# A retention layer and a gated MLP on one core: four more state products as row tiles, k loaded as bf16, stores on a second queue, a new order

## The chip, the core and the metric

The kernel runs on one core of a Trainium2 chip. A core has five engines, each with its own instruction queue that is worked off in order: TensorE (PE: matmuls; its weight loads stand as PEld in the profile), VectorE (DVE), ScalarE (ACT), GpSimd (POOL) and SyncE (SP, which here only issues transfers). They wait for each other through semaphores. Matmuls write to PSUM, eight banks of 128 x 2 KB; the other data lie in SBUF. Transfers run on DMA engines; SP, ScalarE and GpSimd can issue them, and only GpSimd's queue can change the type on the way.

The metric is the device time in microseconds of one execution. The time before is 232.23 us, the median of three runs (232.0 to 232.47).

## What is computed

Two stages, cut to what matters:

```python
# q, k, v: [4 batches, 8 heads, 768 steps, 64]; gamma[h] = 1 - 2**(-5-h)
for t in range(768):
    state = gamma * state + outer(k[t], v[t])         # per batch and head, 64 x 64
    y[t] = (1 / sqrt(64)) * q[t] @ state
x = y as [3072 tokens, 512]
xn = x / sqrt(mean(x * x) + 1e-6) * rms_g
out = (silu(xn @ w_gate) * (xn @ w_val)) @ w_out      # 512 -> 1536 -> 512
```

The inputs and the output are float32 in memory.

## The kernel before

The 768 steps are cut into six chunks (c, 0 to 5) of 128; there are four batches (b, 0 to 3). For each chunk and batch: load q, k and v with decay factors put into them, transpose q and k, form the scores of the chunk (A, L405: 64 rows each, so two heads stand above each other in the array as row tiles), multiply them by a mask on VectorE (M, L427), and add the product of masked scores with v to the product of q with the state of all chunks before (Y, L442 and L446). The state is kept as float32 in `st_f` and as bf16 in `st_b`; K (L529) is k times v, U adds it, B copies it to bf16 on GpSimd. Then the norm: S (square sum, ScalarE, L459), R (the power -1/2, GpSimd, L469 and L471), N (VectorE, L483), and XE transposes the result into `xnT`.

When a chunk's four batches are there (512 tokens), the MLP runs over it: for each of 12 tiles of d_ff, g and v (L553, 4 matmuls of 512 columns each), s (silu on ScalarE, L563), h (the product on VectorE, L571); then for each batch d (12 matmuls, L578), o (copy from PSUM, L145) and st (the store, L591). The MLP of one chunk and the attention of the next are interleaved.

Nothing is scheduled by a compiler. A string ORDER lists some 870 steps; each engine does its own in the order in which they stand there. A step is `name.arguments/banks@engine`, so `A.2.2/7231` makes the scores of chunk 2, batches 2 and 3, in banks 7, 2, 3 and 1, and `st.0.0@S` stores from SP's queue. A step that writes a bank waits until the readers of what was there are done. Names that the change touches:

- Y, plain: 8 matmuls of 128x64 (L442) and 4 of 128x128 (L446), the state as a block diagonal. Where Z stands (L409 to L420; before, for chunk 4, batches 2 and 3 alone), the state product of two batches is made first, as 16 matmuls of 64x64 on row tiles (L418): even heads of both batches in one bank, odd heads in another. Y with a third argument then adds the rest to both banks (L437). S then takes two square sums of 256 columns for each batch (L456), R adds the halves, N writes two halves (L480).
- Lq, Lk, Lv: loads. From SP's queue they bring float32 into a ring (`qf`, `kf`, `vf`); from GpSimd's queue bf16. Ck copies k to bf16 (`kb`), Cq and V put the decay factors into q and v and make bf16 of them. V on ScalarE is 8 instructions (L358), on VectorE or GpSimd one (L360).
- tq, tk: transposes by transfer, from SP's queue.
- H: filler matmuls (L239), 512 columns each, of ones, whose result nobody reads.

Chunk 2's loads wait for the last piece of w_out (`("wo", 8)`); the weights come through GpSimd's queue as bf16, in five pieces each for w_gate and w_val.

Of the kernel before, what the change touches and what calls it, by code (L numbers as in the profile page):

```python
# [22 lines left out]
J.0.3/5 D.0.1@D wv.2.4 R.0.1 X.0.2/6 N.0.1 S.0.0 wg.2.4 A.0.3/41 R.0.0 X.0.1/0 XE.0.2@A wg.4.6 D.0.3@D M0.0.3
XE.0.1@A g.0.0.2.2.3/2 K.0.2.2/5 K.0.0.2/6 M1.0.3 U.0.2.2@A s.0.0.2.2.3 N.0.0 v.0.0.2.2.3/7 g.0.0.2.1.2/0
h.0.0.2.2.3 Y.0.3/5 Lq.1.0@P wv.4.6 X.0.0/3 U.0.0.2@A S.0.3 wg.6.9 Tk.1.1/4 v.0.0.2.1.2/2 XE.0.0@D s.0.0.2.1.2
h.0.0.2.1.2 g.0.0.2.0.1/6 R.0.3 wv.6.9 Ek.1.1@A v.0.3.4.0.3/3 v.0.2.3.0.3/4 N.0.3 g.0.3.4.0.3/0 Lk.1.2@P
s.0.0.2.0.1 X.0.3/6 v.0.0.2.0.1/5 XE.0.3@A Lk.1.0@P B.0.0 wg.9.12 s.0.3.4.0.3 Lq.1.1@P g.0.5.6.0.3/1
g.0.2.3.0.3/7 h.0.3.4.0.3 s.0.2.3.0.3 Lq.1.2@P h.0.2.3.0.3 g.0.4.5.0.3/0 wv.9.12 h.0.0.2.0.1 s.0.4.5.0.3
v.0.0.4.3.4/2 g.0.0.4.3.4/7 v.0.4.5.0.3/3 mc.1@P s.0.5.6.0.3 s.0.0.4.3.4 h.0.0.4.3.4 wo.0.4 v.0.5.6.0.3/4
h.0.5.6.0.3 D.1.1@P Lv.1.1@P h.0.4.5.0.3 Lv.1.0@P g.0.8.9.0.4/7 g.0.6.7.0.4/0 mc.0@D s.0.8.9.0.4 v.0.4.6.3.4/4  # L30
g.0.4.6.3.4/5 s.0.4.6.3.4 v.0.8.9.0.4/6 D.1.0@D D.1.2@P wo.4.8 s.0.6.7.0.4 Tk.1.2/2 Ek.1.2@D Tq.1.0/5
g.0.7.8.0.4/1 Eq.1.0@D h.0.8.9.0.4 v.0.6.7.0.4/7 h.0.4.6.3.4 wo.8.12 v.0.7.8.0.4/3 Lk.2.2@S s.0.7.8.0.4
h.0.6.7.0.4 g.0.11.12.0.4/5 s.0.11.12.0.4 Tk.1.0/7 h.0.7.8.0.4 Lk.2.0@S Tq.1.1/0 Lv.1.2@P Lq.1.3@P Tq.1.2/3
Eq.1.1@D B.0.1 Eq.1.2@D g.0.9.10.0.4/4 s.0.9.10.0.4 B.0.2 g.0.10.11.0.4/2 s.0.10.11.0.4 Ek.1.0@D A.1.0/3710
M1.1.1 A.1.2/46 v.0.10.11.0.4/2 v.0.11.12.0.4/0 M0.1.2 M0.1.1 v.0.9.10.0.4/5 M0.1.0 Lv.2.0@S d.0.0.0.4/1 M1.1.0
M1.1.2 h.0.9.10.0.4 Y.1.1/3 d.0.3.0.4/6 Lk.2.3@S h.0.11.12.0.4 Y.1.0/4 S.1.1 Lk.1.3@P R.1.1 h.0.10.11.0.4 S.1.0
N.1.1 d.0.1.0.4/0 R.1.0 d.0.2.0.4/5 N.1.0 X.1.1/3 d.0.2.4.8 d.0.0.4.8 Lv.1.3@P d.0.3.4.8 X.1.0/7 d.0.3.8.12
XE.1.0@A Y.1.2/2 Tq.1.3/7 d.0.0.8.12 S.1.2 d.0.1.4.8 Lq.2.0@S XE.1.1@D o.0.0@A Eq.1.3@D o.0.3@A R.1.2 N.1.2
Tk.1.3/1 d.0.2.8.12 X.1.2/3 Ek.1.3@A Ck.2.2@P D.1.3@D Lq.2.1@S A.1.3/17 XE.1.2@A M1.1.3 K.1.0/4 K.1.2.2/6
K.1.1/2 B.0.3 M0.1.3 Lq.2.2@S tk.2.2 Ck.2.0@A g.1.0.1.0.3/3 v.1.2.3.0.3/7 U.1.1@D Y.1.3/1 s.1.0.1.0.3  # L40
g.1.1.2.0.3/3 S.1.3 Lk.2.1@S g.1.3.4.0.3/2 o.0.2@A R.1.3 U.1.2.2@D d.0.1.8.12 Cq.2.1@P s.1.3.4.0.3 U.1.0@D
g.1.2.3.0.3/2 v.1.0.1.0.3/5 N.1.3 Lq.3.1@S s.1.1.2.0.3 X.1.3/3 h.1.0.1.0.3 tk.2.0 v.1.3.4.0.3/1 Lk.3.1@S tq.2.1
v.1.1.2.0.3/5 B.1.2 XE.1.3@D h.1.3.4.0.3 Ck.2.3@D s.1.2.3.0.3 h.1.2.3.0.3 h.1.1.2.0.3 g.1.9.10.0.4/4
v.1.9.10.0.4/6 tk.2.3 v.1.0.4.3.4/7 g.1.8.9.0.4/2 Cq.2.0@P Lq.2.3@S o.0.1@D s.1.9.10.0.4 V.2.0@D tq.2.0 Ck.2.1@D
g.1.0.4.3.4/0 B.1.0 v.1.8.9.0.4/5 h.1.9.10.0.4 Cq.2.2@P Lq.3.0@S s.1.0.4.3.4 g.1.11.12.0.4/1 tk.2.1 s.1.8.9.0.4
h.1.0.4.3.4 g.1.5.6.0.4/7 Lv.2.1@S B.1.1 h.1.8.9.0.4 v.1.5.6.0.4/0 s.1.5.6.0.4 g.1.4.5.0.4/4 Ck.3.1@A
g.1.10.11.0.4/5 Cq.3.1@D Lv.2.2@S v.1.11.12.0.4/7 Cq.2.3@P h.1.5.6.0.4 s.1.11.12.0.4 B.1.3 h.1.11.12.0.4
v.1.10.11.0.4/0 s.1.10.11.0.4 s.1.4.5.0.4 h.1.10.11.0.4 v.1.4.5.0.4/4 Cq.3.0@P h.1.4.5.0.4 g.1.7.8.0.4/5
Lk.3.0@S A.2.0/4726 tq.2.3 tq.2.2 M0.2.0 v.1.7.8.0.4/0 Lv.2.3@S tq.3.1 Lk.3.2@S M0.2.1 s.1.7.8.0.4 M1.2.1
g.1.6.7.0.4/1 h.1.7.8.0.4 M1.2.0 V.2.1@P v.1.6.7.0.4/5 Y.2.1/4 Ck.3.0@A s.1.6.7.0.4 S.2.1 K.2.1/0 tk.3.1 K.2.0/6  # L50
V.2.2@P h.1.6.7.0.4 A.2.2/7231 M0.2.3 d.1.1.0.10/5 Lk.3.3@S V.2.3@P M1.2.3 tq.3.0 M1.2.2 d.1.1.10.12 R.2.1
# [588 lines left out]
```

## Time and profile before

| | |
|---|---|
| median of three runs | 232.23 us |
| span of the profiled execution | 230.7 us |
| what lies around the span (median less span) | 1.5 us |
| TensorE busy | 223.7 us, 97% |
| VectorE, GpSimd, ScalarE busy | 128.7, 92.8, 87.8 us |
| bytes moved | 33.60 MB |
| q1 (transfers issued by SP): share of 16 engines | 51.0% |
| q0 (issued by GpSimd): share of 16 engines | 30.3% |

The profiled execution is one more execution; its own time is known by its span, from the first to the last instruction of the program, and the 1.5 us are taken as what lies around it.

How to read the profile: a row of a group has the line, the engine, the operation, what it writes and reads, the shapes and the number of instructions; then busy us in total and the mean ns of one; then the idle time of the engine ahead of them, and what ended it. The view of waits has who waited for whom: us in total, times, the longest. The chain of waits goes from the last instruction back to what released it, step by step; its rows here have start, length and what. In the timeline, a row has start, length, engine, line and operation; matmuls are pipelined, so the length of one holds a tail that overlaps the next, and the pitch is read from start to start.

### The profile page before, as it was taken

How to read it: one execution, taken by the hardware profiler on the slowest of the kernel's cores; microseconds unless marked ns; L12 is line 12 of the kernel's file. 1: busy time of each engine (PE TensorE's matmuls, PEld its weight loads, DVE VectorE, ACT ScalarE, POOL GpSimd, SP SyncE). 2: the span in 40 equal slices, each digit the busy share in tenths (PEclk: the TensorE clock that was granted, in tenths of full speed). 3: DMA queues.
4: the chain of work that ended last, by engine and by line, in shares of the span. 5: the costliest groups of instructions: out<-in, count | busy, mean ns of one | idle time of the engine just before them, and what ended most of it. 6: DMA issues, size and time to landing. Idle time of an engine off the chain costs nothing.

```text
span 230.7 us, 4733 instructions
## 1 busy us (share of the span) xinstructions
PE 223.7 (97%) x1822; PEld 119.3 (52%) x1849; DVE 128.7 (56%) x239; ACT 87.8 (38%) x197; POOL 92.8 (40%) x163
## 2 busy tenths in 40 slices
PE   8989999999999999999999999999999999999994
PEld 2567755556564554445544445544554444444552
DVE  5797296937574876476670648856664325432200
ACT  6776524216424450344420435661354124222021
POOL 8979999124866235424349401339040000000000
PEclk9999999999999999999999999999999999999999
DMA  7999999999978946999999989774216200001142
GB/s 132 158 175 122 187 174 192 201 185 239 180 164 186 203 104 172 245 162 248 231 141 263 216 194 227 155 117 99 65 23 190 108 0 0 0 12 38 45 180 93
DMA packets 105353, 33.60 MB, mean 146 GB/s; under 512 B 94450, under 2 KB 102386, under 8 KB 105331
## 3 DMA queue, kind: packets, MB, share of 16 engines
q1 hardware_dynamic: 81858, 25.70, 51.0%
q0 software_dynamic: 23472, 7.60, 30.3%
q8 instruction: 14, 0.23, 0.4%
q14 instruction: 9, 0.07, 0.1%
HBM read 28.31 MB, written 6.29 MB: 150 GB/s over the span
## 4 chain that ended last, share of the span: by engine, by line
PE 93%; DMA 3%; issue 1%; DVE 1%; ACT 0%; POOL 0%; DVEq 0%
PE v_ps L553 26%; PE g_ps L553 26%; PE o_ps L578 26%; DMA wg_b<-in_moe_w_gate_dram 3%; PE hot_ps L239 3%; PE a_ps L405 3%; PE y_ps L442 2%; PE y_ps L446 2%; PE o_ps L600 1%; PE kv_ps L529 1%; PE t_ps L368 1%; PE t_ps L373 1%; DVE am L427 1%; PE xt_ps L496 1%; PE g_row_ps L295 0%
## 5 line engine op out<-in xcount | busy, mean ns | idle before, releaser
L571 DVE TENSOR_TENSOR hT<-sg,v_ps 128x512 bf16<-128x512 bf16 (+2 forms) x76 | 48.0, 655 | 54.4 <-PE v_ps L553 39.8
L563 ACT ACTIVATE sg<-g_ps 128x512 bf16<-128x512 f32 (+2 forms) x76 | 42.4, 575 | 88.8 <-PE g_ps L553 79.1
L553 PE MATMUL g_ps<-xnT,wg_b 128*128 128x512 bf16 (+2 forms) x334 | 70.2, 343 | 0.8 <-DMA wg_b<-in_moe_w_gate_dram 0.4
L553 PE MATMUL v_ps<-xnT,wv_b 128*128 128x512 bf16 (+2 forms) x338 | 70.4, 344 | 0.5 <-issue 0.2
L578 PE MATMUL o_ps<-wo_b,hT 128*128 128x512 bf16 x265 | 62.3, 379 | 0.6 <-issue 0.2
L553 PEld LDWEIGHTS <-wg_b 128*128 128x128 bf16 x344 | 30.6, 98 | 30.3 <-DMA wg_b<-in_moe_w_gate_dram 0.8
L553 PEld LDWEIGHTS <-wv_b 128*128 128x128 bf16 x344 | 30.5, 98 | 29.1 <-DVE hT L571 0.2
L578 PEld LDWEIGHTS <-hT 128*128 128x128 bf16 x276 | 26.3, 98 | 29.7 <-DVE hT L571 0.2
L469 POOL TENSOR_SCALAR ms<-ssq 128x1 f32<-128x1 f32 x24 | 4.5, 189 | 48.8 <-ACT xsq L459 48.0
L427 DVE TENSOR_TENSOR am<-a_ps,causal 128x512 bf16<-128x512 f32 x32 | 20.2, 682 | 3.3 <-PE a_ps L405 3.2
L483 DVE SCALAR_TENSOR_TENSOR xn<-y_ps,rstd,g_bc 128x512 bf16<-128x512 f32 x22 | 16.4, 748 | 9.8 <-POOL rstd L471 8.0
L545 POOL CAST st_b<-st_f 64x256 bf16<-64x256 f32 x40 | 18.7, 467 | 6.7 <-DVE st_f L538 5.4
L459 ACT ACTIVATE xsq<-y_ps 128x512 f32<-128x512 f32 x22 | 13.1, 598 | 15.6 <-PE y_ps L446 14.2
L341 POOL TENSOR_TENSOR qb<-qf,ydec 128x512 bf16<-128x512 f32 x13 | 13.7, 1055 | 10.5 <-DMA qf<-in_q_dram 10.2
L145 ACT COPY o_sb<-o_ps 128x512 f32<-128x512 f32 (+1 forms) x15 | 8.4, 567 | 23.5 <-PE o_ps L578 23.1
L471 POOL TENSOR_TENSOR rstd<-ms,mhalf 128x1 f32<-128x1 f32 x24 | 13.2, 552 | 2.0
L145 DVE COPY o_sb<-o_ps 128x512 f32<-128x512 f32 (+2 forms) x11 | 6.7, 620 | 13.0 <-PE o_ps L578 7.3
L360 POOL TENSOR_TENSOR vp<-vf,vdec 128x512 bf16<-128x512 f32 x9 | 9.3, 1040 | 5.4 <-DMA vf<-in_v_dram 5.3
L427 DVE TENSOR_TENSOR am<-a_ps,mask 128x512 bf16<-128x512 f32 x16 | 9.9, 681 | 1.6 <-PE a_ps L405 1.4
L239 PE MATMUL hot_ps<-one 128*128 128x512 bf16 x23 | 8.4, 516 | 1.1 <-DVE one L152 1.1
L442 PEld LDWEIGHTS <-am 128*128 128x128 bf16 x176 | 7.7, 98 | 3.5
L442 PE MATMUL y_ps<-vp,am 128*128 128x64 bf16 x176 | 8.8, 193 | 0.0
(98 smaller groups left out, 161.0 us busy)
## 6 DMA issues: line engine op xcount, KB each, us to landing
out_dram<-o_sb SPq DMA_DIRECT2D x23, 256.0 KB, 2.4
kf<-in_k_dram SPq DMA_DIRECT2D x17, 256.0 KB, 3.9
vf<-in_v_dram SPq DMA_DIRECT2D x17, 256.0 KB, 4.4
qf<-in_q_dram SPq DMA_DIRECT2D x16, 256.0 KB, 4.0
wo_b<-in_moe_w_out_dram POOLq DMA_DIRECT2D x3, 512.0 KB, 10.7
qb<-in_q_dram POOLq DMA_DIRECT2D x8, 128.0 KB, 5.8
kb<-in_k_dram POOLq DMA_DIRECT2D x7, 128.0 KB, 7.1
vp<-in_v_dram POOLq DMA_DIRECT2D x7, 128.0 KB, 7.4
```

Of the source, the lines that this page charges most:

```text
L145: (e.copy if e is ACT else e.tensor_copy)(out, in_)
L239: nc.tensor.matmul(p, one, one[:, None, :].to_broadcast([128, 4, 128]), start=True, stop=True)
L341: e.tensor_tensor(out=u["qb"], in0=u["qf"], in1=ydec[:, c, :, None].to_broadcast([128, H, D]), op=ALU.mult)
L427: DVE.tensor_tensor(out=u["am"][:, i], in0=u["a"][i], in1=m, op=ALU.mult)
L442: nc.tensor.matmul(y[:, h, :], u["am"][:, h % 2, h // 2, :], u["vp"][:, h, :], start=h == 0, stop=c == 0 and h == H - 1, skip_group_check= ...
L471: POOL.tensor_tensor(out=u["rstd"], in0=ms, in1=mhalf, op=ALU.pow)
L483: DVE.scalar_tensor_tensor(out=u["xn"], in0=flat(u["y"]), scalar=u["rstd"], in1=g_bc, op0=ALU.mult, op1=ALU.mult)
L545: POOL.tensor_copy(st_b[b][r, :, i * 64:i * 64 + 64], st_f[b // 2][r, b % 2])
L553: nc.tensor.matmul(p[:, (n - n0) * m:(n - n0 + 1) * m], W[w][0][:, s, n * 128:(n + 1) * 128], xnT[c][:, s, b0 * C:b1 * C], start=s == 0, s ...
L563: ACT.activation(sg[:, :cols], done["wg", c, n0, b0][:, :cols], AF.Silu)
L571: DVE.tensor_tensor(out=hT[c][:, n0:n1, b0 * C:b1 * C], in0=sg, in1=p, op=ALU.mult)
L578: nc.tensor.matmul(o_ps[c, b], hT[c][:, n, b * C:(b + 1) * C], wo_b[:, n, :], start=n == 0, stop=n == NFF - 1)
```

## The change

It does five things:

- Z now stands for five pairs of batches instead of one: added are chunks 2, 3 and 4, batches 0 and 1, and chunk 5, batches 2 and 3. Their eight Y become Y with a third argument.
- k of chunks 2 to 5 (16 loads) is loaded by GpSimd's queue as bf16 straight into `kb`. The 16 Ck (7 on ScalarE, 7 on VectorE, 2 on GpSimd) are gone. In `load`, the wait for w_out now holds for loads from SP's queue alone.
- 16 of the 26 stores are issued by ScalarE.
- Some steps change engines: five Cq net go from GpSimd to VectorE, V on ScalarE goes from 2 to 6 (from GpSimd 9 to 6, from VectorE 6 to 5), o on ScalarE from 15 to 19, XE on ScalarE from 5 to 2, the cast of the first k from ScalarE to VectorE.
- ORDER is made anew, with other banks. The fillers H go from 23 matmuls (4, 8, 2, 2, 2, 1, 3, 1) to 11 (2, 2, 2, 2, 3).

Many functions return the instruction that they make, and `load` and D have branches that no step of this order takes: these change nothing that runs. The diff, cut:

```diff
@@ ORDER, the first lines @@
-Lk.0.2@S H.4/4 yd causal Lv.0.2@S>causal yt rms.1@S ident Ck.0.2@A Lq.0.0@P H.8/1 Lq.0.1@P Lq.0.2@P Tk.0.2/7
-H.2/5 Lk.0.0@P Tq.0.1/0 vd Tq.0.0/4 Ek.0.2@D Lk.0.1@P Tq.0.2/1 Lk.0.3@P G/7 V.0.2@D Eq.0.1@D Tk.0.0/0 Tk.0.1/6
+Lk.0.2@S yd causal Lv.0.2@S yt rms.1@S ident Ck.0.2@D Lq.0.0@P H.2/0 Lq.0.1@P Lq.0.2@P Tk.0.2/1 H.2/0 Lk.0.0@P
+Tq.0.1/2 vd Tq.0.0/0 Ek.0.2@D Lk.0.1@P Tq.0.2/1 Lk.0.3@P G/3 V.0.2@D Eq.0.1@D Tk.0.0/2 Tk.0.1/4 Eq.0.2@D Eq.0.0@D iota
...
@@ chunk 2 @@
+Cq.3.1@P h.1.6.7.0.4 tk.2.3 g.1.0.4.3.4/7 Lv.2.0@S tq.3.1 A.2.2/1435 M1.2.2 s.1.0.4.3.4 Z.2.0/26 Y.2.1.2 Lq.3.0@S
+s.1.11.12.0.4 d.1.1.0.10/7 V.2.0@D M0.2.2 S.2.1 M1.2.3 Y.2.0.2 Cq.3.0@P K.2.1/5 K.2.2.2/1 K.2.0/0 M0.2.3 Y.2.3/3 R.2.1
+S.2.3 U.2.1@D U.2.2.2@D S.2.0 st.0.2@A tk.3.1 v.1.11.12.0.4/5 tq.3.0 v.1.0.4.3.4/1 N.2.1 st.0.1@S U.2.0@D Y.2.2/0
...
@@ chunk 5 @@
+d.3.0.10.12 Lq.5.0@S s.4.7.8.0.4 o.2.2@A o.3.1@A Cq.5.0@D B.4.2 tk.5.0 s.4.8.9.0.4 tk.5.3 A.5.2/3751 M1.5.2 Lk.5.1@P
+Cq.5.1@P Lv.5.2@S v.4.8.9.0.4/7 M0.5.3 o.3.0@A Lv.5.3@S tk.5.1 s.4.3.4.0.4 o.3.3@D M0.5.2 V.5.2@P v.4.7.8.0.4/5
...
@@ the last line @@
-d.5.2.0.12/0 st.5.3.2@S st.5.1@S st.5.3.1@S e.5.3.0/1 o.5.2@A st.5.2@S o.5.3.0@A st.5.3.0@S
+o.5.2@D st.4.1@S o.5.3.1@A e.5.3.2/3 e.5.3.0/1 st.5.3.1@A o.5.3.2@D st.5.3.2@A o.5.3.0@A st.5.3.0@A st.4.0@S st.5.2@S
@@ load @@
-            x = t[c, b][n + "f"] = ring([128, H, D], F32, n + "f", {"q": 4, "k": 4, "v": 6}[n])
-        if n != "v" and c == 0 and e is POOL and not near:
+            x = t[c, b][n + "f"] = ring([128, H, D], F32, n + "f", RING[n])
+        if n != "v" and c == 0 and (near == 8 if e is SP else not near):
...
-        elif c == 2:
+        elif c == 2 and e is SP:
             after(i, ("wo", 8))
```

More of the change, by code (lines that the diff above doesn't have):

```diff
@@ L23 @@
[L23 to L27, printed above, removed]
@@ L144, in copy @@
     def copy(e, out, in_):
-        (e.copy if e is ACT else e.tensor_copy)(out, in_)
+        return (e.copy if e is ACT else e.tensor_copy)(out, in_)
     def flat(x):
@@ L242, in iota @@
     def iota(e, bk):
-        POOL.affine_select(out=row_m, in_=row_f, compare_op=ALU.is_ge, fill=1.0e6, base=0,
+        return POOL.affine_select(out=row_m, in_=row_f, compare_op=ALU.is_ge, fill=1.0e6, base=0,
                            pattern=[[1, C]], channel_multiplier=-1)
@@ L257, in vd @@
     def vd(e, bk):
-        ACT.activation(vdec, darg, AF.Exp, scale=-1.0, bias=zero)
+        return ACT.activation(vdec, darg, AF.Exp, scale=-1.0, bias=zero)
     @op
     def yd(e, bk):
-        ACT.activation(ydec, darg, AF.Exp, scale=1.0, bias=lnscale)
+        return ACT.activation(ydec, darg, AF.Exp, scale=1.0, bias=lnscale)
     def mask(i):
@@ L280, in mc @@
         dec = vdec[:, 1].rearrange("p (hp i) -> p hp i", i=2)[:, :, i:i + 1]
-        e.tensor_tensor(out=mask1[:, i], in0=causal[:, None, :].to_broadcast([128, NHP, C]),
+        return e.tensor_tensor(out=mask1[:, i], in0=causal[:, None, :].to_broadcast([128, NHP, C]),
                         in1=dec.to_broadcast([128, NHP, C]), op=ALU.mult)
@@ L285, in tab @@
     def tab(e, bk):
-        ACT.activation(warm, zero, AF.Silu)
+        return ACT.activation(warm, zero, AF.Silu)
     @op
@@ L298, in GE @@
     def GE(e, bk):
-        copy(e, g_bc, done["G"])
+        return copy(e, g_bc, done["G"])
     def load(n, e, c, b, near=0):
@@ L426, in M @@
         m = (mask0, mask1)[c][:, i] if c <= 1 else causal[:, None, :].to_broadcast([128, NHP, 128])
-        DVE.tensor_tensor(out=u["am"][:, i], in0=u["a"][i], in1=m, op=ALU.mult)
+        return DVE.tensor_tensor(out=u["am"][:, i], in0=u["a"][i], in1=m, op=ALU.mult)
     F["M0"] = lambda e, bk, c, b: M(0, c, b)
@@ L458, in S_ @@
         u["ssq"] = ring([128, 1], F32, "ssq", 4)
-        ACT.activation(xsq, flat(u["y"]), AF.Square, accum_out=u["ssq"])
+        return ACT.activation(xsq, flat(u["y"]), AF.Square, accum_out=u["ssq"])
     @op
@@ L470, in R @@
         u["rstd"] = ring([128, 1], F32, "rstd", 4)
-        POOL.tensor_tensor(out=u["rstd"], in0=ms, in1=mhalf, op=ALU.pow)
+        return POOL.tensor_tensor(out=u["rstd"], in0=ms, in1=mhalf, op=ALU.pow)
     @op
@@ L482, in N @@
             return
-        DVE.scalar_tensor_tensor(out=u["xn"], in0=flat(u["y"]), scalar=u["rstd"], in1=g_bc,
+        return DVE.scalar_tensor_tensor(out=u["xn"], in0=flat(u["y"]), scalar=u["rstd"], in1=g_bc,
                                  op0=ALU.mult, op1=ALU.mult)
@@ L501, in XE @@
         if e is SP:
-            SP.dma_start_transpose(out=x, in_=t[c, b]["xn"])
+            return SP.dma_start_transpose(out=x, in_=t[c, b]["xn"])
         else:
-            copy(e, x, t[c, b]["xP"])
+            return copy(e, x, t[c, b]["xP"])
     @op
@@ L535, in U @@
         if c == 0:
-            copy(e, x, t[c, b]["kv"])
+            return copy(e, x, t[c, b]["kv"])
         else:
-            DVE.tensor_tensor(out=x, in0=x, in1=t[c, b]["kv"], op=ALU.add)
+            return DVE.tensor_tensor(out=x, in0=x, in1=t[c, b]["kv"], op=ALU.add)
     @op
@@ L562, in s_ @@
         sg = done["s", c, n0, b0] = ring([128, GT], BF16, "sg", 3)
-        ACT.activation(sg[:, :cols], done["wg", c, n0, b0][:, :cols], AF.Silu)
+        return ACT.activation(sg[:, :cols], done["wg", c, n0, b0][:, :cols], AF.Silu)
     @op
@@ L570, in h_ @@
         sg, p = (done[w, c, n0, b0][:, :(n1 - n0) * m].rearrange("p (n t) -> p n t", t=m) for w in ("s", "wv"))
-        DVE.tensor_tensor(out=hT[c][:, n0:n1, b0 * C:b1 * C], in0=sg, in1=p, op=ALU.mult)
+        return DVE.tensor_tensor(out=hT[c][:, n0:n1, b0 * C:b1 * C], in0=sg, in1=p, op=ALU.mult)
     @op
```

163 lines of the change are left out of this document (80 added, 83 removed).

## The prediction

> **What bounds the kernel now.** I read the page first, then the clock, then what TensorE waited for, then the chain of waits in order of time, then the timeline of the first 24 us.
>
> ```profile
> span 230.7 us, 4733 instructions
> PE 223.7 (97%) x1822; PEld 119.3 (52%) x1849; DVE 128.7 (56%) x239; ACT 87.8 (38%) x197; POOL 92.8 (40%) x163
> PE 93%; DMA 3%; issue 1%; DVE 1%; ACT 0%; POOL 0%; DVEq 0%
> ```
>
> TensorE sets the time: 97% busy, 93% of the chain. What TensorE itself waited for is short; the longest of it, once real work has begun, in the view of waits (total, times, longest):
>
> ```profile
> PE g_ps L553 <- DMA wg_b<-in_moe_w_gate_dram: 0.4, 1, 0.4
> ```
>
> So once the weights flow there is nothing left to hide: whatever makes TensorE wait is added in full, and only fewer or shorter matmuls, or an earlier start, can gain. In the chain of waits (start, length, what) the first 23 us are the other stage:
>
> ```profile
> 1.11 5.30 PE hot_ps L239 x12
> ...
> 7.34 1.08 PE t_ps L368 x48
> 8.43 1.05 PE g_row_ps L295 x2
> 9.48 0.80 PE t_ps L368 x32
> 10.28 0.35 PE a_ps L405 x8
> 10.73 1.90 DVE am L427 x3
> ...
> 15.63 0.52 POOL rstd L471
> 16.16 6.63 DMA wg_b<-in_moe_w_gate_dram
> 22.83 0.82 PE g_ps L553 x4
> ```
>
> A string of short matmuls leads to a mask product, a norm (rstd), and only then does GpSimd, whose queue is in order, issue the weight transfer at 16.16 that lands when TensorE needs it. Lateness before 16.16 is passed on through that transfer.
>
> **Row tiles.** Four pairs of batches (batches 0 and 1 of chunks 2, 3 and 4, batches 2 and 3 of chunk 5) change from 2 x 4 matmuls of 128x128 to 16 of 64x64. The kernel before has both kinds; the timeline gives starts:
>
> ```profile
> 149.11 0.41 PE L418 MATMUL y_ps<-st_b,qT 64*128 64x64 bf16 x16
> 149.45 1.04 PE L553 MATMUL v_ps<-xnT,wv_b 128*128 128x512 bf16 x3
> ...
> 168.80 0.39 PE L446 MATMUL y_ps<-st_b,qT 128*128 128x128 bf16 x4
> 169.02 1.03 PE L553 MATMUL v_ps<-xnT,wv_b 128*128 128x512 bf16 x4
> ```
>
> From start to next start the 16 tiles take 0.34; in the old form a batch takes 0.22 and a pair 0.44: 0.10 saved, 0.40 for four. In the changed order all four new products stand next to the score products (L405), which are row tiles already; should they share the change of mode, some 0.10 more each is saved, 0.80 in all (an estimate: 16 tiles at about the 16 ns that remain). I take -0.5, ends 0 and -0.8. The Trainium skill (TensorE: Matmul & The Clock Gate, Part 3: Packing small matmuls) has tiles of different row groups run together for little more than the time of one; by it a pair would take half of 0.44, and the term would be -0.9. The row is 0.34, so the trace bears out only a part of that.
>
> The price is that two batches now share two PSUM banks. The square sum of each batch becomes two of 256 columns, the norm too, and GpSimd adds the halves:
>
> ```profile
> L459 ACT ACTIVATE xsq<-y_ps 128x512 f32<-128x512 f32 x22 | 13.1, 598 | 15.6 <-PE y_ps L446 14.2 <-PE y_ps L442 1.3
> L459 ACT ACTIVATION_READ_ACCUMULATOR xsq<-y_ps 128x1 f32 x22 | 4.4, 199 | 0.0
> L456 ACT ACTIVATE xsq<-y_ps 128x256 f32<-128x256 f32 x4 | 1.5, 391 | 0.0
> L456 ACT ACTIVATION_READ_ACCUMULATOR xsq<-y_ps 128x1 f32 x4 | 0.9, 218 | 0.0
> L480 DVE SCALAR_TENSOR_TENSOR xn<-y_ps,rstd,g_bc 128x256 bf16<-128x256 f32 x4 | 1.8, 480 | 2.1 <-POOL rstd L471 2.1
> L538 DVE TENSOR_TENSOR st_f<-st_f,kv_ps 128x512 f32<-128x512 f32 (+1 forms) x10 | 5.5, 573 | 2.7 <-PE kv_ps L529 2.7
> ```
>
> Busy, that is 8 x (2 x 0.61 - 0.80) = 3.4 us more on ScalarE, and some on VectorE, behind 38% and 56% load. The new wait is the matter. Its cover comes in such pieces (the chain again):
>
> ```profile
> 163.70 0.86 PE v_ps L553 x4
> ...
> 165.02 0.55 PE a_ps L405 x16
> ```
>
> In the changed program the norm of chunk 2, batch 1 waits, besides its own rstd, for the square sums of batch 0, which read the same banks. On ScalarE those stand behind the square sum of batch 3, which waits for batch 3's y product on TensorE. On VectorE the state update of batch 0 is queued behind that norm; it frees bank 0, and TensorE's y product of batch 2 goes into bank 0. After batch 3's product TensorE has two v groups for cover, 0.86 each, 1.7. The way round: the latency of the last matmul, about 0.2; the square sum of batch 3 and the two halves of batch 0, 0.80 + 2 x 0.61 less some 0.1 of overlap each, 1.7; the second half of the norm 0.48; the update of one batch, under the row's mean of 0.57, say 0.4. That is 2.8, with hand-overs, against 1.7. Take +0.9, ends 0 (should the queues stand earlier than I think) and 1.4.
>
> **A bank taken straight back.** In the new order, right behind the score products of chunk 5, batches 2 and 3, TensorE goes on with a v group (d_ff tile 8 of chunk 4) in bank 7, where half of batch 2's scores have just been written. It must wait for that half's mask product:
>
> ```profile
> L427 DVE TENSOR_TENSOR am<-a_ps,causal 128x512 bf16<-128x512 f32 x32 | 20.2, 682 | 3.3 <-PE a_ps L405 3.2
> ```
>
> The half is whole 0.27 (half of 0.55) before the 16 end; then latency of 0.2, the product 0.68, a hand-over: +0.6, ends 0 and 0.8.
>
> **The fillers.** L239's matmuls go from 23 to 11: ahead of the first transposes 2 instead of 12, 2 behind them as before, later 7 instead of 9. The old ones kept TensorE to 6.41. That brings nothing, since the next products wait for q, which is there at 7.34 whatever the fillers do, and the later ones stood in waits: 0 for their own time (ends -0.5, 0.3). What they did besides is in the clock and the timeline:
>
> ```profile
> core 0: 230.7 us, clock 1.000
> ```
>
> ```profile
> 5.78 0.63 PE L239 MATMUL hot_ps<-one 128*128 128x512 bf16 x1
> 6.93 0.38 PE L239 MATMUL hot_ps<-one 128*128 128x512 bf16 x1
> 7.34 0.97 PEld L368 LDWEIGHTS <-qb 128*64 128x64 bf16 x48 [0.56 <-DMA qb<-in_q_dram]
> 14.38 1.24 PE L239 MATMUL hot_ps<-one 128*128 128x512 bf16 x5
> ```
>
> The twelve at the head run one in 0.43 (5.30 for 12, less the last one's tail), the five at 14.38 one in 0.215. TensorE began at half speed and reached full speed between 5.78 and 6.93, some 5.2 us after it began to work, although the granted clock is 1.000 throughout. With 2 fillers it has 0.9 us of work at 1.1 us and 1.3 us when the first k is there (the transposes and two more), then waits for q. Unbroken work begins at 7.34; at the same 5.2 us, full speed comes near 12.5. The four pieces from 7.34 to 10.63 are 3.28 us long without a gap; at half speed until 12.5 they hold 2.6 of it, the rest follows, and the scores are done 2.6 us later. That passes through the mask products and the rstd to the weight transfer, TensorE's next wait. Ends: 0, if the broken work counts; 2.8, if the later matmuls before 14 us suffer too. Nothing points to one end; I take the middle, +1.4. By the Trainium skill (same page, Part 1: The HAM clock gate) the clock is gated to one half until a free-running window of about 3.4 us was busy, so 3.4 to 6.8 us after dense work begins; the 5.2 of the trace agrees, and by the rule the term would be between 1.7 and 2.8.
>
> **k through GpSimd, stores through ScalarE, the rest of the order.**
>
> ```profile
> kf<-in_k_dram SPq DMA_DIRECT2D x17, 256.0 KB, 3.9
> kb<-in_k_dram POOLq DMA_DIRECT2D x7, 128.0 KB, 7.1
> L314 POOL DMA_DIRECT2D kb<-in_k_dram x4 | 3.6, 909 | 0.0
> L358 ACT ACTIVATE vp<-vf,vdec 128x64 bf16<-128x64 f32 x16 | 4.0, 347 | 0.0
> L314 SPq DMA_DIRECT2D kf<-in_k_dram x17: 392/573/1903, 0.8 to 134.6; - x17
> ```
>
> 16 casts leave ScalarE, VectorE and GpSimd; 16 issues of 0.91 us (14.5 us) come to GpSimd, 40% busy, which loses two of the casts, five q and three v products. The loads land 3 us later than from SP's queue (7.1 against 3.9), but nearly all are issued long before the transposes that read them. SP's queue loses 32 issues. ScalarE gets 16 stores, and at SP's median of 0.57 an issue I take 9 us; it gets four more v scalings of eight pieces, 2 us each (4.0 for 16), and four copies of results, and loses eight casts and three copies. At 38% the load fits; but a v scaling in front of a silu (L563) holds back the bank that the silu frees. With 1.7 us of TensorE per g and v group and eight banks, one 2 us hold is covered, two with a store between are not: 0, ends -0.3 and +3. The tail ends with the same 192 columns, copied and stored by ScalarE: 0.
>
> **Sum.** -0.5 + 0.9 + 0.6 + 1.4 = +2.4 on a span of 230.7, 233.1. The span lies 1.5 us under the runs' median of 232.23; with the same 1.5 the time is 234.6.
>
> **Rivals.**
> (1) Faster: full speed comes as early as before and both waits are covered, so the row tiles are what is left, with 0.4 of the fillers: 232.23 - 0.5 - 0.4, about 231.3. For it: queues that lose 32 issues and 16 casts, so every load is earlier. Against it: the 0.43 a filler at the head, and a chain without slack up to 16.16. It decides if the scores of batch 2 of chunk 0 begin before 10.7.
> (2) The change doesn't do what it says: with the mode's change paid each time the tiles save 0.4, and a late start of about 0.5 gives it back: 232.3.
> (3) ScalarE becomes the queue that TensorE waits for: v scalings and stores ahead of silus, in chunks 3 to 5, add 2.5 to the forecast: 237.1. For it: four holds of 2 us that were not there. Against it: 38% load.
>
> **How the numbers follow.** Forecast 0.55, faster 0.17, no net effect 0.12, ScalarE 0.16. This measurement can tell about 0.2% (0.46 us) from no change. Forecast and ScalarE are slower but for the low tail, where the clock term and one wait are nothing; that gives slower 0.71, same 0.12, faster 0.17. The range runs from 231.5 (most of rival 1 and all of rival 2 are within or near it) to 237.2. The forecast's own range, from its terms, is 233.0 to 236.2.
>
> **What would show it.** The starts of the fillers and of L368's groups after 7.3 us: pitch of 0.43 and doubled groups until about 12. The scores of batch 2 near 12 to 13 instead of 10.28, the weight transfer at 17 to 18.5 instead of 16.16. A TensorE wait of 0.5 to 1.3 on VectorE's st_f ahead of the plain y product near 84 us, and one near 0.6 on am ahead of v_ps near 167. The y product's tiles: 0.24 to 0.34 for 16. I am wrong if TensorE runs at full speed at 8 us, if those two waits are missing, or if TensorE waits for ScalarE's sg or vp by over 1 us.

## The result and the profile after

The changed kernel takes 235.82 us (median of 4 runs, 235.42 to 235.85); the kernel before, run beside it, 232.12 us (231.87 to 232.47). The ratio is 1.0138, with a 95% interval of 1.0108 to 1.0169: slower by 1.4%. (The two medians are 3.70 us apart, 1.6%; why the ratio lies lower is not shown.) The forecast was 234.6, with a range of 231.5 to 237.2. Ratios leave out runs over 1.5% above the fastest of the same kernel, so where a kernel's runs spread further than that, its ratio reads lower than its median.

The page of the changed kernel, the span and the engines:

```profile
span 234.1 us, 4825 instructions
PE 223.5 (95%) x1869; PEld 118.7 (51%) x1869; DVE 129.6 (55%) x243; ACT 92.3 (39%) x239; POOL 98.8 (42%) x177
```

TensorE is busy for as long as before (223.5 against 223.7 us), and the span is 3.4 us longer. The busy times match although ten fillers at the head are gone, since the real work after them is done at half speed; the rest of the lost time is waiting. The view of waits of TensorE (us in total, times, longest):

```profile
PE t_ps L369 <- DVE kb L140: 2.6, 1, 2.6
PE t_ps L364 <- DMA qb<-in_q_dram: 1.6, 1, 1.6
PE y_ps L438 <- DVE st_f L534: 0.8, 1, 0.8
PE v_ps L549 <- DVE am L423: 0.6, 1, 0.6
```

The last two are the waits that the prediction named. The first two are the gaps at the start that the fillers used to fill. What follows from these gaps is in the timeline (start, length, engine, line, work) of the changed kernel's start:

```profile
5.16 1.06 PE L234 MATMUL hot_ps<-one 128*128 128x512 bf16 x2
7.84 1.49 PE L364 MATMUL t_ps<-pick,qb 128*64 128x64 bf16 x48 [1.62 <-DMA qb<-in_q_dram]
9.26 2.07 PE L290 MATMUL g_row_ps<-g_row,ones 1*128 1x512 f32 x2
12.27 1.46 PE L401 MATMUL a_ps<-qT,kT 64*128 64x128 bf16 x24
13.66 0.64 PE L364 MATMUL t_ps<-pick,kb 128*64 128x64 bf16 x16
14.34 0.41 PE L438 MATMUL y_ps<-vp,am 128*128 128x64 bf16 x8
18.07 0.81 POOL L321 DMA_DIRECT2D wg_b<-in_moe_w_gate_dram  x1
23.36 1.46 PE L549 MATMUL v_ps<-xnT,wv_b 128*128 128x384 bf16 x8
```

The 48 transposes take 1.49 instead of 1.08 us and the two scale-row products 2.07 instead of 1.12 (timeline of the kernel before): TensorE runs at half speed until about 14 us. Only the scale-row products double; the transposes take 1.4 times as long, and the 24 scores 1.46 us against 1.15 at full speed (e1). The scores of batch 2 begin at 12.27 instead of 10.28 (as the chain before has it), the weight transfer goes out at 18.07 instead of 16.16. The last row is a good mark, since both kernels have it; in the kernel before it stands here:

```profile
20.94 1.46 PE L553 MATMUL v_ps<-xnT,wv_b 128*128 128x384 bf16 x8
```

So 2.4 of the 3.4 us are lost by then. The two waits follow, first that of chunk 2 (timeline of VectorE and TensorE), then that of chunk 5 (chain of waits: start, length, what):

```profile
85.20 0.88 DVE L476 SCALAR_TENSOR_TENSOR xn<-y_ps,rstd,g_bc 128x256 bf16<-128x256 f32 x2 [1.08 <-ACT xsq L452]
85.99 0.41 DVE L534 TENSOR_TENSOR st_f<-st_f,kv_ps 128x256 f32<-128x256 f32 x1
86.45 0.39 PE L438 MATMUL y_ps<-vp,am 128*128 128x64 bf16 x8 [0.75 <-DVE st_f L534]
```

```profile
151.72 0.02 DVE xn L476
...
167.48 0.35 PE a_ps L401 x8
...
167.85 0.70 DVE am L423
...
168.60 1.89 PE v_ps L549 x8
```

The norm of batch 1 waits for ScalarE's square sum (xsq), the state update stands behind it, and the y product behind that. At 168 us the chain goes through VectorE's mask product: TensorE wanted the bank straight back. The piece at 151.72 is a third one, which the prediction did not have: an output product (L575) waits until the norm has read a bank that a pair shared. It starts 0.72 us after the products ahead of it; where no pair shares the bank (e12), it starts after 0.48, so the wait is 0.24.

### The profile page after: what moved, and what is told of

It is laid out like the page before. It is cut to its first block, busy times and chain, and to the rows that moved or that the text cites. A ratio compares the mean times of both kernels' runs of the same rounds, so it can differ in the third digit from the quotient of the medians.

```text
span 234.1 us, 4825 instructions
## 1 busy us (share of the span) xinstructions
PE 223.5 (95%) x1869; PEld 118.7 (51%) x1869; DVE 129.6 (55%) x243; ACT 92.3 (39%) x239; POOL 98.8 (42%) x177
## 5 line engine op out<-in xcount | busy, mean ns | idle before, releaser
L575 PE MATMUL o_ps<-wo_b,hT 128*128 128x512 bf16 x276 | 63.7, 379 | 0.1
L575 PEld LDWEIGHTS <-hT 128*128 128x128 bf16 x276 | 26.3, 98 | 29.6 <-issue 0.2
L140 ACT COPY o_sb<-o_ps 128x512 f32<-128x512 f32 (+1 forms) x19 | 10.3, 560 | 33.1 <-PE o_ps L575 28.8
L309 POOL DMA_DIRECT2D kb<-in_k_dram x20 | 18.3, 918 | 0.0
L337 POOL TENSOR_TENSOR qb<-qf,ydec 128x512 bf16<-128x512 f32 x8 | 8.3, 1043 | 21.6 <-DMA qf<-in_q_dram 21.5
L455 ACT ACTIVATE xsq<-y_ps 128x512 f32<-128x512 f32 x14 | 8.4, 599 | 23.0 <-PE y_ps L442 21.1
L479 DVE SCALAR_TENSOR_TENSOR xn<-y_ps,rstd,g_bc 128x512 bf16<-128x512 f32 x14 | 10.4, 747 | 6.8 <-POOL rstd L467 6.6
L354 ACT ACTIVATE vp<-vf,vdec 128x64 bf16<-128x64 f32 x48 | 12.0, 338 | 0.7 <-DMA vf<-in_v_dram 0.7
L140 DVE COPY o_sb<-o_ps 128x512 f32<-128x512 f32 (+1 forms) x7 | 4.4, 632 | 13.5 <-PE o_ps L575 8.1
L337 DVE TENSOR_TENSOR qb<-qf,ydec 128x512 bf16<-128x512 f32 x8 | 7.0, 893 | 8.7 <-DMA qf<-in_q_dram 8.7
L476 DVE SCALAR_TENSOR_TENSOR xn<-y_ps,rstd,g_bc 128x256 bf16<-128x256 f32 x20 | 8.6, 478 | 4.8 <-POOL rstd L467 3.7
L356 POOL TENSOR_TENSOR vp<-vf,vdec 128x512 bf16<-128x512 f32 x6 | 6.2, 1040 | 11.8 <-DMA vf<-in_v_dram 11.8
```

The costliest lines, as they stand in the source:

```text
L140: return (e.copy if e is ACT else e.tensor_copy)(out, in_)
L309: i = done[n, c, b] = e.dma_start(out=x, in_=rows[n][b, c])
L337: e.tensor_tensor(out=u["qb"], in0=u["qf"], in1=ydec[:, c, :, None].to_broadcast([128, H, D]), op=ALU.mult)
L354: ACT.activation(u["vp"][:, h], u["vf"][:, h], AF.Copy, scale=vdec[:, c, h:h + 1])
L479: return DVE.scalar_tensor_tensor(out=u["xn"], in0=flat(u["y"]), scalar=u["rstd"], in1=g_bc, op0=ALU.mult, op1=ALU.mult)
L575: nc.tensor.matmul(o_ps[c, b], hT[c][:, n, b * C:(b + 1) * C], wo_b[:, n, :], start=n == 0, stop=n == NFF - 1)
```

## The experiments

A run's span is cut in two at the mark above: "start" is when the first v group of 384 columns begins, "rest" is the span less that. Medians are over all runs of a kernel, start and rest are those of its profiled execution. The runs come in groups, each with the kernel before beside it; its medians were 232.12 (beside the changed kernel), 232.42 (e1 to e4, e9, e10), 232.13 (e5 to e8) and 232.5 (e11, e12), so differences of under 0.4 us between kernels of different groups are not read.

| kernel | median us (runs) | ratio, 95% interval | start | rest |
|---|---|---|---|---|
| before | 232.1 to 232.5 | 1 | 20.94 | 209.8 |
| changed | 235.82 (4) | 1.0138, 1.0108 to 1.0169 | 23.36 | 210.7 |
| e1: changed, 12 head fillers | 233.87 (9) | 1.0060, 1.0044 to 1.0076 | 20.99 | 211.2 |
| e2: before, 2 head fillers | 234.97 (10) | 1.0075, 1.0039 to 1.0110 | 24.50 | 209.8 |
| e3: changed, two waits removed | 234.62 (4) | 1.0095, 1.0061 to 1.0130 | 22.95 | 210.0 |
| e4: e1 and e3 | 233.67 (10) | 1.0059, 1.0036 to 1.0083 | 22.12 | 211.3 |
| e5: e4, first mending | 233.67 (8) | 1.0060, 1.0038 to 1.0081 | 20.64 | 211.2 |
| e6: e5 without the four pairs | 235.70 (5) | 1.0153, 1.0130 to 1.0176 | 20.72 | 213.0 |
| e7: e5, stores on SP | 235.95 (4) | 1.0170, 1.0133 to 1.0208 | 21.11 | 212.6 |
| e8: before, k by GpSimd | 233.38 (5) | 1.0058, 1.0032 to 1.0085 | 20.97 | 210.7 |
| e9: e5, second mending | 231.87 (12) | 0.9978, 0.9951 to 1.0004 | 21.09 | 209.3 |
| e10: e9 without the four pairs | 234.22 (12) | 1.0070, 1.0048 to 1.0092 | 21.25 | 210.4 |
| e11: changed, 6 head fillers | 235.37 (7) | 1.0092, 1.0056 to 1.0129 | 22.41 | 211.3 |
| e12: e9 without two of the pairs | 231.92 (12) | 0.9973, 0.9956 to 0.9991 | 20.85 | 209.2 |

**e1, the head fillers back.**

```diff
-Lq.0.0@P H.2/0 Lq.0.1@P
+Lq.0.0@P H.12/0 Lq.0.1@P
```

> The changed kernel with 12 fillers ahead of the first transposes again, as the kernel before had (2 before). Clock theory (TensorE runs at half speed until it has worked some 5.2 us, and the short head put that off): full speed before 7 us, the transposes of q from 7.8 us on at a pitch as in the kernel before, the two scale-row matmuls in 1.1 instead of 2.1 us, the weight transfer issued near 16.5 instead of 18.1 us; the time falls by 1.9 us (1.5 to 2.4; about 0.5 of the 2.4 us lateness at the start is q's later landing, which stays), to about 233.9. Rival (the new order's queues on GpSimd and VectorE are late at the start, whatever TensorE's clock): no change within 0.3 us, and the weight transfer still at 18.

Measured: 233.87, 1.95 less. Timeline of e1's start:

```profile
1.11 4.69 PE L234 MATMUL hot_ps<-one 128*128 128x512 bf16 x12 [1.11 <-DVE one L147]
6.99 1.06 PE L364 MATMUL t_ps<-pick,qb 128*64 128x64 bf16 x48 [0.54 <-DMA qb<-in_q_dram]
7.98 1.12 PE L290 MATMUL g_row_ps<-g_row,ones 1*128 1x512 f32 x2
```

Full speed from the transposes on, and the mark is back at the time of the kernel before (20.99 against 20.94). Not all of the 2.4 us that the start gained is the clock: q also landed earlier in this execution (the transposes begin at 6.99 instead of 7.84), which the expectation had taken to stay late. The whole gained less than the start did, since the rest grew by 0.5. The waits of e1 show why:

```profile
PE a_ps L401 <- DMA kT<-kb: 1.2, 1, 1.2
PE y_ps L438 <- DVE st_f L534: 0.7, 1, 0.7
```

Now 2.4 us earlier, TensorE reaches the scores of chunk 5, batches 2 and 3 before their transposed k is there. The wait for the mask product is gone by itself, since the scores come in two pieces. SP had issued that transposition 2.4 us earlier too (162.59 instead of 164.95), but it took 3.9 us to land instead of 2.4. Each window of e1 has here its bounds, its length, busy us of PE, PEld, DVE, ACT and POOL, the granted clock, the DMA share and GB/s:

```profile
163.00:164.00 1.00, 1.00 (x7) 0.41 (x5) 0.00 (x0) 1.00 (x3) 0.67 (x1) 1.00 3.69 193
164.00:165.00 1.00, 1.00 (x7) 0.34 (x7) 0.00 (x0) 0.84 (x2) 0.36 (x1) 1.00 0.13 6
```

For about a microsecond all transfers stood nearly still (6 GB/s) with several under way. In the changed kernel the same k had landed at 167.32, 0.1 us before its scores began at 167.41: that slack was all there was.

**e2, the kernel before with a short head.**

```diff
-Lk.0.2@S H.4/4 yd ... Lq.0.0@P H.8/1 Lq.0.1@P
+Lk.0.2@S H.2/4 yd ... Lq.0.0@P Lq.0.1@P
```

> The kernel before with 2 fillers ahead of the first transposes instead of 12, nothing else. Clock theory: the pieces from 7.3 to 10.6 us take about 1.5 us longer, the weight transfer goes out 1.5 to 2 us later, the time rises by 1.6 to 2.4 us, to about 234.0. Rival (head fillers do nothing but fill): the first transposes start at about 4.8 instead of 6.2 us, the q transposes still wait for q, no change within 0.3 us.

Measured: 234.97, but the ten runs lie between 232.07 and 236.24; those of e1 between 233.49 and 234.47. The profiled one is the slowest, its rest that of the kernel before to 0.1 us. All its loss is at the start:

```profile
8.07 1.49 PE L368 MATMUL t_ps<-pick,qb 128*64 128x64 bf16 x48 [1.27 <-DMA qb<-in_q_dram]
...
16.07 0.60 PE L368 MATMUL t_ps<-pick,qb 128*64 128x64 bf16 x16
24.50 0.81 PE L553 MATMUL v_ps<-xnT,wv_b 128*128 128x384 bf16 x4
```

Ten filler matmuls that nobody reads are worth 3.6 us in this execution: 0.73 of it is q's later landing (8.07 instead of 7.34), 2.8 the slower work from there to the mark. The cause is not the new order, since nothing else of it is here. The spread suggests that the price depends on something that differs from run to run; only one run of each kernel has a profile, so that the other runs lost their time at the start is not shown.

**e3, the two waits taken away.**

```diff
-U.2.1@D U.2.2.2@D S.2.0 ... N.2.1 st.0.1@S U.2.0@D Y.2.2/0
+U.2.1@D U.2.2.2@D U.2.0@D S.2.0 ... N.2.1 st.0.1@S Y.2.2/0
-A.5.2/3751 M1.5.2 ... v.4.8.9.0.4/7 ... o.3.3@D ... g.4.0.1.0.4/0
+A.5.2/3751 o.3.3@D M1.5.2 ... g.4.0.1.0.4/0 v.4.8.9.0.4/7
```

> The changed kernel with two waits taken away: the state update of chunk 2, batch 0 stands ahead of the norm of batch 1 in VectorE's queue; behind the score products of chunk 5, batches 2 and 3, TensorE does a g group in bank 0 first (its copy to be emptied moved up), and only then the v group in bank 7. Theory of the two waits: TensorE's waits of 0.8 us on st_f and 0.6 us on am are gone from the view of waits, and the end comes 1.4 us earlier (0.9 to 1.5), about 234.4. Rival (the time comes back in a later wait, since TensorE was ahead of its inputs): both rows gone, others grown, 0 to -0.4.

Measured: 234.62, 1.2 less. Both rows are gone from the view of waits, and one is new:

```profile
PE g_ps L549 <- ACT sg L560: 0.6, 1, 0.6
```

The start was 0.4 earlier than in the changed kernel by itself; 0.4, 0.8 and 0.6 less the new 0.6 make the 1.2. So both waits were real, and the rival was right in part: one of them came back in another place, made by my exchange of the groups (the silu of the g group put first has to wait for a buffer).

**e4, both together.**

> Both edits together: the long head and the two waits taken away. If the parts add up: -3.3 us (2.6 to 3.9), about 232.5, level with the kernel before within 0.5 us; what the row tiles gain (0.8) is then used up by q's late landing at the start (0.5) and small waits (0.4). Rival (ScalarE's stores and v scalings or GpSimd's loads are what makes the new order slow): 234.5 or more.

Measured: 233.67, 2.15 less instead of 3.3. Its waits:

```profile
PE a_ps L401 <- DMA kT<-kb: 1.0, 1, 1.0
PE g_ps L549 <- ACT sg L560: 0.6, 1, 0.6
```

The two are 1.6 us and more than make up what is missing. The profiled execution (235.1, the slowest of ten) lost another 1.1 us at the start. One window of it, columns as above:

```profile
12.00:13.00 1.00, 0.83 (x24) 0.70 (x22) 1.00 (x2) 0.97 (x2) 0.72 (x1) 0.50 1.88 154
```

The granted clock is 0.50 here, and so it is to 15 us: after being at full speed TensorE was throttled again.

**e5, the first mending.** To e4: the transposition of k of chunk 5, batch 3 ahead of two q loads in SP's queue; three groups in other banks.

```diff
-tq.5.3 Lq.5.1@S d.3.0.10.12 Lq.5.0@S ... tk.5.0 s.4.8.9.0.4 tk.5.3 A.5.2/3751
+tq.5.3 tk.5.3 Lq.5.1@S d.3.0.10.12 Lq.5.0@S ... tk.5.0 s.4.8.9.0.4 A.5.2/3751
-g.4.0.1.0.4/0 v.4.8.9.0.4/7 ... v.4.7.8.0.4/5 ... h.4.7.8.0.4 s.4.0.1.0.4 h.4.8.9.0.4
+v.4.8.9.0.4/0 ... v.4.7.8.0.4/7 g.4.0.1.0.4/5 ... h.4.8.9.0.4 h.4.7.8.0.4 s.4.0.1.0.4
```

> The kernel with both edits (long head, two waits taken away), and what these laid bare mended: TensorE then waited 1.0 to 1.2 us for a transposed k of chunk 5 (kT<-kb), whose transfer stands behind two q loads in SP's queue, and 0.6 us for a silu (sg) after my exchange of groups. The transposes of chunk 5, batch 3 now stand ahead of the two q loads; the v groups of d_ff tiles 8 and 7 take banks 0 and 7, the g group of tile 0 bank 5. If the lost time is the clock and waits alone: no TensorE wait over 0.3 us after 24 us, 1.6 us less than with both edits, about 232.0, so level with the kernel before or up to 0.8 us (the row tiles) faster. Rival (the new queues on ScalarE and GpSimd cost time elsewhere): 233.2 or more, with new waits on kT, kb, vp or sg.

Measured: 233.67, nothing gained. The waits for kT and sg are gone, but a new one stands at the same place, as the waits and VectorE's timeline show:

```profile
PE v_ps L549 <- DVE o_sb L140: 1.9, 1, 1.9
```

```profile
165.22 0.69 DVE L337 TENSOR_TENSOR qb<-qf,ydec 128x512 bf16<-128x512 f32 x1 [9.70 <-issue]
165.83 0.68 DVE L140 COPY o_sb<-o_ps 128x512 f32<-128x512 f32 x1
```

The q load that I put back by a transposition comes later (counted from each run's mark, SP issues it 1.25 us later than in e4); VectorE, which is in order, waits for it, and behind it stands the copy that empties TensorE's next bank. "Issue" in brackets means that the profile names no releaser; that it was the load is read from the order and removed in e9.

**e6, e5 without the four pairs.** The four Z are taken out, and Y.c.b.2 becomes Y.c.b with a bank of its own.

> The mended kernel with the four added row-tile state products taken back: eight plain y products (8 matmuls of 128x64 and 4 of 128x128 each), in the banks that the pairs used. Theory of shared mode change (a pair costs about 0.24 next to score products, 0.44 plain): 0.8 us slower than the mended kernel (0.5 to 1.0). Rival 1 (the change of mode is paid each time, 0.34 a pair): 0.4 slower. Rival 2 (ScalarE's and VectorE's extra pieces for the halved norms cost as much as the tiles save): level or faster.

Measured: 235.70, 2.0 slower than e5. It does not measure the tiles, since waits of its own came with it (TensorE for qT 1.0 us, and two of 0.2 to 0.3 at the scores of chunk 3); hence e10 and e12.

**e7, stores on SP.** The 16 `st` with @A get @S.

> The mended kernel with the 16 stores issued by SP again, at the same places in the order. Main theory (ScalarE has room for them): level within 0.3 us, or slower where a store that waits for its result now holds up loads and transposes behind it on SP. Rival (stores on ScalarE delay the silus and square sums that TensorE needs): 0.5 to 2.5 us faster.

Measured: 235.95, slower by 2.3, not faster. Up to TensorE's last matmul e7's profiled execution is 0.45 behind e5's; the rest is the tail. SP's row of e7 and ScalarE's last of e5:

```profile
224.49 6.26 SPq L588 DMA_DIRECT2D out_dram<-o_sb  x8
```

```profile
229.02 0.34 ACTq L588 DMA_DIRECT2D out_dram<-o_sb  x1
```

Eight stores go out one behind the other on one queue, until 230.75, instead of 229.36. The 0.45 is there by the mark already (21.11 against 20.64), so in the body nothing is gained by taking the stores off ScalarE; at the end two queues help. (The order was made for two queues: SP waits here for results in another sequence.)

**e8, k by GpSimd alone.** In the kernel before, Lk of chunks 2 to 5 becomes @P, the 16 Ck go, and the wait for w_out in `load` holds for SP's loads alone.

> The kernel before with one part of the change: k of chunks 2 to 5 loaded by GpSimd as bf16 at the places where SP loaded it, the 16 casts gone; the order otherwise as before. Main theory (this part is hidden): level with the kernel before within 0.4 us. Rival (GpSimd's 16 issues of 0.9 us delay its v scalings, state copies and powers, or k comes late): 1 us or more slower, with TensorE waits on kT, st_b or xn.

Measured: 233.38, ratio 1.0058: 1.3 us slower, the rival's side. The loss is in the rest (+0.9), in small TensorE waits between 35 and 56 us, the largest of which is:

```profile
PE kv_ps L529 <- DMA vp<-in_v_dram: 0.4, 1, 0.4
```

TensorE waits for v of chunk 1, batch 3, which comes through GpSimd's queue as well. At the old places k loads stand ahead of it: it is issued when it was before (46.83 against 46.92), but lands after 9.2 us instead of 4.9. The changed kernel's order has other places for both and shows no such wait.

**e9, the second mending.** The two q loads of chunk 5 go out right behind the first one, some 15 us earlier, and the copy stands ahead of VectorE's q product, which had waited for the load:

```diff
-S.4.1 Lq.5.2@S st.2.1@A ... o.3.1@A Cq.5.0@D
+S.4.1 Lq.5.2@S Lq.5.1@S Lq.5.0@S st.2.1@A ... o.3.1@A o.3.3@D Cq.5.0@D
```

> The mended kernel once more, since my mending made a wait of its own: with the k transposes put ahead of them, two q loads of chunk 5 landed later, VectorE stood 1.3 us longer for one of them, and the copy that empties TensorE's next bank was queued behind (v_ps on o_sb, 1.9 us). Now the two q loads are issued some 15 us earlier, while SP waited anyway, and the copy stands ahead of the product that waited. If TensorE is otherwise fed: that wait gone, no TensorE wait over 0.4 us after 24 us, 1.9 us less than 233.67, so 231.8, between 0.8 us faster than and level with the kernel before. Rival (every wait that is taken away is replaced by another, since the order has no slack in chunk 5): 233 or more.

Measured: 231.87, 1.8 less than e5, as expected. No TensorE wait over 0.3 is left after 24 us:

```profile
PE v_ps L549 <- DVE hT L568: 0.3, 1, 0.3
```

The ratio of 0.9978 still has 1 within its interval (0.9951 to 1.0004): level with the kernel before, perhaps 0.5 us faster.

**e10, e9 without the four pairs.**

> That kernel with the four added row-tile products taken back. In the first such pair TensorE's own progress showed 0.2 us for each pair, but two waits of 0.7 and 1.2 us for chunks 3 and 5 stood beside it. Shared mode change: 0.8 us slower (0.5 to 1.1) than the kernel with row tiles, plus waits, named, on qT or sg; mode paid each time: 0.4 slower; tiles worth nothing: level.

Measured: 234.22, 2.35 slower by the medians; by the profiled executions 1.2 (its own is the fastest of 12). What TensorE itself needs is read from start to start. Chunk 2 in e9, then, without the pair, in e12:

```profile
77.25 0.62 PE L401 MATMUL a_ps<-qT,kT 64*128 64x128 bf16 x16
77.71 0.40 PE L414 MATMUL y_ps<-st_b,qT 64*128 64x64 bf16 x16
78.04 0.41 PE L433 MATMUL y_ps<-vp,am 128*128 128x64 bf16 x8
80.77 0.70 PE L525 MATMUL kv_ps<-vp,kb 128*64 128x64 bf16 x32
```

```profile
76.56 0.62 PE L401 MATMUL a_ps<-qT,kT 64*128 64x128 bf16 x16
77.11 0.41 PE L438 MATMUL y_ps<-vp,am 128*128 128x64 bf16 x8
80.28 0.69 PE L525 MATMUL kv_ps<-vp,kb 128*64 128x64 bf16 x32
```

The scores take 0.46 where the pair follows and 0.55 where a plain product does; with 0.33 of the pair, 0.79 against 0.55: a pair costs 0.24 beside scores, where two plain products cost 0.44. From scores to kv it is 3.52 against 3.72: 0.20 saved. The pairs of chunks 3, 4 and 5 in e9 read alike: 0.78 to 0.79 for pair and scores, against the 0.99 of scores and two plain products.

**e11, six fillers.** To the changed kernel: `H.2/0` at the head becomes `H.6/0`.

> The changed kernel with 6 fillers at the head instead of 2 (12 gave 233.87). The fillers then run from 1.1 to 3.7 us, and TensorE stands still for about 1 us until the first k is there. If all work counts, wherever it lies, 5.2 us of it are done by about 8.4 us: full speed from there, and about 1.4 of the 2 us of the 12 fillers, 234.4. If only unbroken work counts (my reckoning in the prediction), full speed still comes near 12 us and nothing is gained, 235.8. A dependence on where fixed stretches of time begin would show as a spread of over 1 us between runs.

Measured: 235.37; the seven runs lie between 233.20 and 236.86. The profiled one:

```profile
1.11 2.74 PE L234 MATMUL hot_ps<-one 128*128 128x512 bf16 x6 [1.11 <-DVE one L147]
6.90 1.50 PE L364 MATMUL t_ps<-pick,qb 128*64 128x64 bf16 x48 [0.68 <-DMA qb<-in_q_dram]
12.72 0.64 PE L364 MATMUL t_ps<-pick,kb 128*64 128x64 bf16 x16
```

Still half speed at 12.7 us, so work ahead of the two gaps (0.9 us for k, 0.7 for q) did not count in this execution; and the spread that the third sentence of the expectation asked for is there.

**e12, two pairs taken back** (chunks 2 and 4), to settle what e10 left.

> The kernel of the last mending (231.87) with the row-tile products of chunks 2 and 4 alone taken back, those of chunks 3 and 5 kept. Shared mode change: 0.2 us a pair, 0.4 slower, about 232.3, and no wait on kT or qT that the mended kernel lacks. If taking back all four cost 2.35 us because plain products are dearer than the 0.2 that TensorE's progress shows: 1.2 slower, about 233.0.

Measured: 231.92, level with e9 (0.05). The 2.35 of e10 therefore lie with chunks 3 and 5, where plain products come with a wait for kT (0.3 in e10's profile, at chunk 3); the 1.1 by which the medians differ more than the profiled executions were not seen in a profile and stay open. That the expected 0.4 is not to be seen has two parts in the traces: the pair of chunk 4 also brings the 0.24 behind the norm, which e12 does not have, and the 0.2 that this leaves of two pairs is below what two medians here can tell. e12's interval, 0.9956 to 0.9991, is the only one wholly under 1.

## Why the prediction was right, and where its sum was off

It named slower at 71%, and the mechanisms stood where it put them: the scores at 12.27 and the weight transfer at 18.07, both waits and the tiles' 0.24 to 0.34 lie within the signs that it had named. The time came out 1.2 above the 234.6.

- **The clock, +1.4, measured +1.9: the term that was mis-sized.** The mark came 2.4 later, of which 0.5 is q's landing (below). From the first of q's transposes to the mark it is 15.52 us in the changed kernel and 15.51 in e11, against 13.57 to 13.61 in e5, e6, e7 and e12, the same order at full speed (e1 has 14.00, with a wait of 0.3 for k): 1.9. e1 and e2 show the cause from both sides. The reckoning itself gave 2.6, and two errors in it went against each other, which is luck. It let every piece double, but only the scale-row products did. And it had full speed 5.2 us after unbroken work begins; it came after 5.8 to 6.5 (between 13.66 and 14.34). The 1.4 was the middle between 0 and 2.8, taken without a reason for it. The end "0, if the broken work counts" was a real one for single runs: e2's fastest run is as fast as the kernel before. That the four runs of the changed kernel lie within 0.43 us, while e2's and e11's spread over 4.2 and 3.7, is not explained.
- **q's landing, not in the sum, measured +0.5.** The transposes begin at 7.84 instead of 7.34. It lies between 6.90 and 8.07 in the executions quoted, so this is chance of the execution as far as is known.
- **The Trainium skill** (TensorE: Matmul & The Clock Gate, Part 1: The HAM clock gate) gave 1.7 to 2.8 for this term, and the 1.9 lies in it. (Redone by the same reckoning, the upper end is 3.3: all 3.28 us of pieces at half speed.) Its free-running window of 3.4 us would also make the price differ from run to run, as in e2 and e11; no run here tests that. Not all agrees: in e12 full speed came after about 2.7 us of work, where the rule has at least 3.4, and in e2 TensorE worked without a break to speak of from 8.07 until full speed near 16.6, 8.5 us, where the rule has at most 6.8.
- **The wait at chunk 2, +0.9, measured 0.75,** with the queue (norm, then update, then y product) as told. Its own pieces gave 2.8 less 1.7, that is 1.1; 0.9 was a choice. Moving the update ahead removed it (e3).
- **The bank taken straight back, +0.6, measured 0.56,** removed in e3 as well.
- **Row tiles, -0.5, measured -0.8** on TensorE (four times 0.20). The estimate that neighbouring scores share the change of mode was right. Missing were two waits beside the pairs: 0.24 ahead of an output product in chunk 4, the price of sharing a bank, and 0.3 at chunk 5. There the changed kernel's pair has its scores 0.55 after it, where e9 has 0.25:

```profile
173.00 0.41 PE L414 MATMUL y_ps<-st_b,qT 64*128 64x64 bf16 x16
173.55 0.62 PE L401 MATMUL a_ps<-qT,kT 64*128 64x128 bf16 x16
```

The profile names no releaser; the last transposed q of these scores was issued at 171.05 and landed after 2.4 us, so it is likely that one, but no run shows it for this kernel.

- **k and stores, 0.** Right for the changed kernel: after 24 us its view has no wait for kT, kb, sg or vp. But "nearly all are issued long before" is the new order's doing; at the old places the k loads cost 1.3 (e8). As for rival 3, ScalarE's queue, e7 settles it for the stores; the v scalings there were not tested alone.
- **What lies around the span, 1.5, measured 1.75** (235.85 less 234.1). For the kernel before it was too low as well: in its later runs, which list their spans, time less span is 1.83 to 2.00. Its profiled execution of 230.7 thus lay somewhat above its median, and the spans differ by 0.3 less than the medians.

Together 1.9 + 0.5 + 0.75 + 0.56 - 0.8 + 0.24 + 0.3 are 3.45, the whole of the 3.4 within rounding. Rival 1 named the start of the scores before 10.7 as its point of decision; it was 12.27. Rival 2's late start of 0.5 was 2.4.

The experiments add what the prediction did not see: the changed order has hardly any slack near 165 us. Lateness of 2.4 at the start hid a transfer that came 0.1 us ahead of its use; with the start mended, three waits took each other's place there until the loads were issued 15 us earlier (e9).

## What to carry to other kernels

Filler work ahead of the first real work is judged by when full speed comes, not by its own time: compare start-to-start times of equal matmuls at the start, and never by one run, since the runs of one kernel with a short head lay up to 4.2 us apart (e2). A reordered kernel is judged at its end and at a mark past its start; when lateness at the start is removed, look for transfers and in-order queues that had just kept up. Where two results come to share a bank, list every reader that must be done and what stands behind it in its queue.

## What was not expected

- The granted clock in the rows is no test of half speed. Between 7 and 14 us of the changed kernel it reads 1.000 while the 24 score products take 1.46 us, against 1.15 in e1; in e4 it reads 0.50 for the same slowness (16 transposes in 0.64 us in both, against 0.44 at full speed).
- How long TensorE works before full speed differs from run to run. At the head of e12 the twelve fillers took 4.10 us, which by a pitch of 0.43 and then 0.215 puts the change after about 6 of them, 2.7 us; in the kernel before it came between 5.78 and 6.93, 4.7 to 5.8 us after the first; in e2 it took 8.5 us.

```profile
1.11 4.10 PE L234 MATMUL hot_ps<-one 128*128 128x512 bf16 x12 [1.11 <-DVE one L147]
```

- In e1 all transfers of the core stood nearly still for about 1.3 us, from 163.9. This began half a microsecond after a 16 KB transfer of instructions; that the one makes the other was not tested.
